# Sharing two of 64 dv stores unequally among the 16 DMA engines, and spreading six dk stores in place of seven, in an attention backward kernel bound by DMA

## The chip, the cores and the metric

The kernel runs on one core of a Trainium2 chip. The metric is the device time of one execution in microseconds, as the median of repeated runs. The core has 16 DMA engines. TensorE is PE in the profile (its weight loads are PEld), VectorE is DVE, ScalarE is ACT, GpSimd is POOL and SyncE is SP. The experiments had their own runs of the kernel before on the same chip, 9 to 11 of them per group, with medians of 1288.36, 1288.98, 1289.48, 1288.53 and 1289.18 us, so every measurement is given as a ratio as well. Differences between medians of different groups are good to 1 or 2 us: the 17.4 us below are 16.4 by the ratios.

## The reference

The reference is the forward and backward pass of attention with one query per head: 2 x 32 = 64 heads, 8192 keys, a head size of 128, all bf16.

```python
scores = jnp.einsum("bhqd,bhkd->bhqk", q, k) * q.shape[-1] ** -0.5
out = jnp.einsum("bhqk,bhkd->bhqd", softmax(scores), v)
# returned: out and the gradients dq, dk, dv for grad_out
```

With one query per head, dk and dv are outer products as large as k and v. Each head reads 2 MB of k and 2 MB of v, and writes 2 MB of dk and 2 MB of dv. That is 268 MB read and 268 MB written for very little arithmetic.

## The kernel before

A k or v tile has 128 rows (partitions) of 16 KB. SyncE issues all the big loads, on one queue; GpSimd issues all the big stores, on another. VectorE writes dk and dv over k and v in the same tile. There are 12 such tiles, six heads' worth, so a load must wait until the store of the tile's former owner has landed.

```python
def slot_of(i, w):          # w = 0: k, then dk; w = 1: v, then dv
    n = 2 * i + w
    return n if n < NTILE else slot_of(i - NTILE // 2, 1 - w)

def by_rows(eng, dst, src, rows):
    p = 0
    for m in rows:
        pin(eng.dma_start(out=dst[p : p + m], in_=src[p : p + m], max_dma_last_dim=NT * D))
        p += m
# ... (cut: load() issues the k or v tile of head i on SyncE)
            dst = (dv_v if w else dk_v)[i]
            if w == 0 and i in SPREAD:          # SPREAD = range(5, 64, 9): seven heads
                by_rows(store_eng, dst, h.tile[w], (P - 2, 2))
            else:
                pin(store_eng.dma_start(out=dst[:, b0:b1, :], in_=h.tile[w][:, b0:b1, :]))
```

So k of head i + 6 is loaded into the tile from which dv of head i is stored, and the wait stands in SyncE's program order.

The Trainium skill ("DMA: Bandwidth & Descriptors", section "Why a DMA increments its semaphore by 16 and not by 1") says that a transfer uses the largest number of engines, up to 16, that divides its outermost size. For GpSimd they are consecutive from a cursor that goes round; for SyncE they are the lowest-numbered ones. By that, 126 rows go to 14 engines with 9 rows each and the 2 rows that follow go to the remaining two, which so write 1 row where a plain store gives every engine 8. I call such a store a spread store. The packet records of the trace agree in number: 14 series of 18 half-row packets, and two engines without. The records carry no engine numbers, so every engine number in this document rests on that rule and on the cursor that the kernel sets to 6 at its start.

## Time and profile before

| | before |
|---|---|
| time, median of 3 runs | 1288.93 us (1288.64 to 1291.01) |
| HBM traffic over the span | 416 GB/s |
| last v load issued / last store issued | 1215.2 / 1279.0 us |
| landing of a 2 MB store / a k load | 67.1 / 21.1 us |

These lines are from the page of the kernel before: the rates in 40 equal slices, and the DMA issues with their size and the median time from issue to landing.

```profile
span 1290.8 us, 42577 instructions
...
DMA  9999999999999999999999999999999999999994
GB/s 390 423 427 428 427 427 426 428 427 427 427 427 428 428 426 425 412 429 426 428 426 427 427 426 428 428 426 424 426 427 428 426 421 424 427 429 426 421 383 185
...
HBM read 268.47 MB, written 268.47 MB: 416 GB/s over the span
...
out_dram<-kvt POOLq DMA_DIRECT2D x119, 2048.0 KB, 67.1
kvt<-in_v_dram SPq DMA_DIRECT2D x64, 2048.0 KB, 20.9
kvt<-in_k_dram SPq DMA_DIRECT2D x63, 2048.0 KB, 21.1
```

The rate stands near 427 GB/s from the third slice to the 38th (412 at the least), then falls to 383 and 185. One store and one load are issued about every 9.8 us, so by these landing times (67.1 / 9.8 and 21 / 9.8) some seven stores and two loads are in flight.

The waits view of the kernel before (waiting engine and line, what it waited for, us in total, times, longest):

```profile
PE tp L184 <- DMA kvt<-in_v_dram: 75.4, 43, 5.1
PE tp L184 <- DMA kvt<-in_k_dram: 23.7, 31, 2.0
```

SyncE's timeline of the kernel before around 500 us, and its last load (start, us, engine, line, transfer):

```profile
502.97 0.33 SPq L98 DMA_DIRECT2D kvt<-in_k_dram  x1
512.82 0.33 SPq L98 DMA_DIRECT2D kvt<-in_v_dram  x1
523.43 0.33 SPq L98 DMA_DIRECT2D kvt<-in_k_dram  x1
539.62 0.33 SPq L98 DMA_DIRECT2D kvt<-in_v_dram  x1
544.81 0.33 SPq L98 DMA_DIRECT2D kvt<-in_k_dram  x1
```

### The profile page before, as it was taken

Reading aid. Unit: us, or ns where it says so; the run is one execution under the profiler, and the core shown is the slowest. Engines: PE = TensorE matmul, PEld = TensorE weight load, DVE = VectorE, ACT = ScalarE, POOL = GpSimd, SP = SyncE. Lnnn points to the kernel's source line nnn. Section 1 sums busy time; section 2 is a strip of 40 time slices with the busy share of each in tenths; the row PEclk is TensorE's granted clock in tenths of the full one; section 3 lists DMA queues with packets and bytes.
Section 4 is the critical chain, followed back from the end, with each engine's and each line's share of the span. In section 5 each row is a group of like instructions: output and inputs, shape, how many; then the busy total and the mean of one; then the engine's idle time right before and its main releaser. Section 6 shows DMA issues by size and latency. Waiting matters only on the chain.

```text
span 1290.8 us, 42577 instructions
## 1 busy us (share of the span) xinstructions
PE 1126.7 (87%) x19268; PEld 856.4 (66%) x19268; DVE 936.1 (73%) x2122; ACT 975.1 (76%) x641; POOL 79.3 (6%) x150
## 2 busy tenths in 40 slices
PE   6999999988998988989888889899898888988870
PEld 5777777666676766766666667677666666766650
DVE  2888888777787777767667777677677776777780
ACT  6888888777787777777778777778687777877740
POOL 0000000000000000000000000000000000000000
PEclk9999999999999999989999998899899999999985
DMA  9999999999999999999999999999999999999994
GB/s 390 423 427 428 427 427 426 428 427 427 427 427 428 428 426 425 412 429 426 428 426 427 427 426 428 428 426 424 426 427 428 426 421 424 427 429 426 421 383 185
DMA packets 39985, 539.67 MB, mean 418 GB/s; under 512 B 5116, under 2 KB 5116, under 8 KB 6396
## 3 DMA queue, kind: packets, MB, share of 16 engines
q0 software_dynamic: 20784, 268.45, 49.4%
q1 hardware_dynamic: 19020, 268.51, 48.8%
q8 instruction: 150, 2.46, 0.7%
q14 instruction: 31, 0.25, 0.0%
HBM read 268.47 MB, written 268.47 MB: 416 GB/s over the span
## 4 chain that ended last, share of the span: by engine, by line
DMA 37%; another core or an unknown queue 27%; PE 20%; DVE 7%; issue 5%; ACT 1%; SPq 1%; POOL 0%; POOLq 0%; ACTq 0%
DMA kvt<-in_v_dram 17%; DMA kvt<-in_k_dram 13%; PE tp L184 9%; DMA out_dram<-kvt 6%; PE acc L339 5%; DVE kvt L394 4%; PE dpw L195 3%; PE sw L195 2%; DVE sel L362 1%; ACT ev L186 1%; SPq L98 1%; PE dpw L282 1%; DMA qd_nat<-in_q_dram 1%; DVE sel L356 0%
## 5 line engine op out<-in xcount | busy, mean ns | idle before, releaser
L186 ACT COPY ev<-tp 128x2048 bf16<-128x2048 bf16 x512 | 954.3, 1865 | 269.2 <-PE tp L184 257.6
L184 PE MATMUL tp<-ident_bf,kvt 128*128 128x128 bf16 x8192 | 556.0, 222 | 99.2 <-DMA kvt<-in_v_dram 75.4
L394 DVE TENSOR_TENSOR kvt<-qb,pair 128x2048 bf16<-128x2048 bf16 x512 | 621.4, 1214 | 0.3
L184 PEld LDWEIGHTS <-kvt 128*128 128x128 bf16 x8192 | 486.4, 100 | 106.7 <-DMA kvt<-in_v_dram 79.1
L195 PEld LDWEIGHTS <-ev 128*128 128x128 bf16 x8192 | 243.1, 96 | 208.1 <-issue 150.5
L339 PE MATMUL acc<-kvt,dS_pad 128*64 128x512 bf16 x1024 | 167.3, 409 | 1.6 <-DVE dqT L379 1.6
L339 PE MATMUL acc<-kvt,E_pad 128*64 128x512 bf16 x1024 | 160.5, 394 | 0.0
L195 PE MATMUL dpw<-qdT,ev 128*128 128x1 bf16 x4096 | 140.8, 164 | 17.6 <-DVE qb L177 16.6
L362 DVE SCALAR_TENSOR_TENSOR sel<-acc,diag,sel 128x128 f32<-128x128 f32 x384 | 134.7, 351 | 13.6
L195 PE MATMUL sw<-qdT,ev 128*128 128x1 bf16 x4096 | 141.8, 164 | 1.1 <-ACT ev L186 1.1
L411 POOL DMA_DIRECT2D out_dram<-kvt x127 | 68.0, 535 | 1121.0 <-DVE kvt L394 950.5
L207 DVE TENSOR_REDUCE mp<-sw 128x1 f32<-128x64 f32 x64 | 14.4, 224 | 149.7 <-PE sw L195 149.7
L339 PEld LDWEIGHTS <-dS_pad 128*64 128x64 bf16 x1024 | 37.6, 111 | 25.1 <-issue 5.1
L247 DVE CAST E_pad<-E_f 128x64 bf16<-128x64 f32 x64 | 12.5, 195 | 55.5 <-ACT E_f L238 55.5
L339 PEld LDWEIGHTS <-E_pad 128*64 128x64 bf16 x1024 | 36.3, 108 | 21.1 <-issue 0.4
L253 DVE CUSTOM_DVE_ANT_0 junk<-E_f,dpw 128x64 bf16<-128x64 f32 x64 | 14.1, 221 | 48.9 <-PE dpw L195 48.9
L376 PE MATMUL acc<-ones,sel 128*128 128x1 f32 x256 | 43.4, 239 | 6.2 <-DVE sel L362 6.2
L282 PE MATMUL dpw<-ld,ones 128*128 128x1 f32 x256 | 46.3, 250 | 0.1
L356 DVE TENSOR_SCALAR sel<-acc,diag 128x128 f32<-128x128 f32 x128 | 44.1, 344 | 0.0
L376 PEld LDWEIGHTS acc<-ones,sel 128*128 128x128 f32 x256 | 39.1, 193 | 7.3 <-DVE sel L362 7.3
L177 DVE CAST qb<-dpw 128x128 bf16<-128x128 f32 x128 | 35.5, 277 | 6.0 <-PE dpw L168 6.0
L282 PEld LDWEIGHTS dpw<-ld,ones 128*128 128x128 f32 x256 | 38.2, 189 | 0.5 <-DVE ld L253 0.5
(44 smaller groups left out, 313.3 us busy)
## 6 DMA issues: line engine op xcount, KB each, us to landing
out_dram<-kvt POOLq DMA_DIRECT2D x119, 2048.0 KB, 67.1
kvt<-in_v_dram SPq DMA_DIRECT2D x64, 2048.0 KB, 20.9
kvt<-in_k_dram SPq DMA_DIRECT2D x63, 2048.0 KB, 21.1
out_dram<-kvt POOLq DMA_DIRECT2D x7, 2016.0 KB, 70.6
out_dram<-kvt POOLq DMA_DIRECT2D x8, 512.0 KB, 22.2
kvt<-in_k_dram SPq DMA_DIRECT2D x2, 512.0 KB, 4.4
kvt<-in_k_dram SPq DMA_DIRECT2D x1, 1024.0 KB, 7.0
out_dram<-kvt POOLq DMA_DIRECT2D x7, 32.0 KB, 70.6
```

The lines of the kernel that those rows point to most:

```text
L177: pin(nc.vector.tensor_copy(out=h.qb[w][:], in_=h.qbp))
L184: pin(nc.tensor.transpose(tp[:, t, :], src[:, c * CH + t, :], ident_bf[:]))
L186: pin(nc.scalar.copy(out=ev[:], in_=tp[:]))
L195: nc.tensor.matmul(dst[:, c * CH + t : c * CH + t + 1], lhsT=ev[:, t, :], rhs=qdT[:, w, i : i + 1], start=True, stop=True,)
L207: pin(nc.vector.reduce_max(out=h.mp[:], in_=h.s, axis=AX.X))
L282: nc.tensor.matmul(out, lhsT=ones[:].to_broadcast([P, P]), rhs=col, start=True, stop=True)
L339: nc.tensor.matmul(h.acc[w][g : g + CW, :], lhsT=wts[:, n0 : n0 + CW], rhs=rows[:, n0 : n0 + QT, :].rearrange("p n d -> p (n d)"), start=( ...
L356: nc.vector.tensor_scalar(out=h.sel[:], in0=block, scalar1=diag[:, 0:1], scalar2=None, op0=ALU.mult)
L362: nc.vector.scalar_tensor_tensor(out=h.sel[:], in0=block, scalar=diag[:, b : b + 1], in1=h.sel[:], op0=ALU.mult, op1=ALU.add,)
L376: nc.tensor.matmul(h.acc[w][:, 0:1], lhsT=h.sel[:], rhs=ones[:], start=True, stop=True)
L394: nc.vector.tensor_tensor(out=h.tile[w][:, n0 : n0 + CH, :].rearrange("p n (e t) -> p n e t", t=2), in0=h.qb[w][:] .rearrange("p (e t) -> ...
L411: pin(store_eng.dma_start(out=dst[:, b0:b1, :], in_=h.tile[w][:, b0:b1, :]))
```

## The change

Engines do not come out even. By the reading of the packet records in the prediction below, eight of them also fetch instructions, which costs each some 25 us over the run (an estimate), and one engine is slow throughout. The intent of the change was to give more of two dv stores to engines thought to be free of that: 19 rows to each of the engines 14, 15 and 0 to 3, the rest to be shared so that the cursor comes out where it was. One dk spread store was dropped and the others moved.

```diff
-SPREAD = range(5, 64, 9)
+NARROW = (22, 44)
+SPREAD = range(7, 64, 10)
...
+    def narrow(dst, src):
+        m = 6 * 19
+        def eighths(ap, h):
+            parts = ap[P - 1 : P].rearrange("p (e h n) d -> p h e (n d)", e=8, h=2)
+            return parts[:, h]
+        pin(store_eng.dma_start(out=eighths(dst, 0), in_=eighths(src, 0)))
+        for r in (slice(0, m), slice(m, P - 1, P - 2 - m)):
+            pin(store_eng.dma_start(out=dst[r], in_=src[r], max_dma_last_dim=NT * D))
+        pin(load_eng.dma_start(out=eighths(dst, 1), in_=eighths(src, 1)))
+        for j in range(1, 5):
+            r = slice(m + j, P - 2, 4)
+            pin(load_eng.dma_start(out=dst[r], in_=src[r], max_dma_last_dim=NT * D))
...
-            if w == 0 and i in SPREAD:
+            if w == 1 and i in NARROW:
+                narrow(dst, h.tile[w])
+            elif w == 0 and i in SPREAD:
```

GpSimd stores half of the last row in eight pieces (to move the cursor by 8), then 114 rows on six engines, then 2 rows. SyncE stores the other half row and the 11 rows left over.

## The prediction

> **What bounds the kernel.** DMA traffic. The page's GB/s row stands near 427 in nearly every slice from 30 to 1,190 us, all 16 DMA engines busy; PE is busy 87%, ACT 76%, DVE 73%. 536.9 MB at 427 GB/s is 1,257 us; the remaining 34 us are the start (about 10) and the tail: the last two slices show 383 and 185 GB/s. Only the tail can be won, and it is set by the DMA engine that is latest with its own backlog.
>
> I read this from the trace's packet records. A 16 KB row packet takes 0.611 us, and the next on that engine starts 0.607 us later; until 1,240 us 16 packets are in flight, so they can be strung into 16 chains, one per engine:
> - Eight engines take the 150 instruction-fetch packets in turn. Each takes 0.97 us and stretches its neighbour to 0.98, so it costs about 1.3 us: some 25 us per engine over the run.
> - One of the two engines that the old spread stores relieve has packets of 0.63 to 0.65 us throughout: some 50 us.
> - The rest run clean. At the last spread store (head 59) they finish 32 us before the fetching ones, and one fetching engine is 7 us later still. At the end one engine alone writes for 6 us, after 10 us with 3 to 7 engines busy. Idle time after 1,240 us adds up to 276 engine-us: perfect balance can win 17 us.
>
> **What the change moves.** The Trainium skill ("DMA: Bandwidth & Descriptors", "Why a DMA increments its semaphore by 16 and not by 1") says that a transfer uses the largest count up to 16 that divides its outermost size, on consecutive engines from a cursor for GpSimd, on the lowest-numbered for SyncE. Before's packet sizes agree with 14 engines for 126 rows (18 half-row packets on 14 chains, 2 on two). By it, in 16 KB rows: engines 6 to 13 lose 17 each (-10.3 us); 3, 14, 15 gain 21 (+12.7), 2 gains 27, 0 and 1 gain 29 (+17.6); 4 and 5 lose 7 (-4.2). Bytes and compute are unchanged. This helps if the fetching engines are mostly 6 to 13; the clean ones have room (over 25 us). The records carry no engine numbers; I infer this from the change's intent, about 3 in 4. If fetching engines lie among 0 to 3, 14 and 15, the end moves about 10 us later.
>
> **Cost.** The narrow store's remainder goes through SyncE, in order: the next load (same buffer) waits until those rows land behind loads in flight (21 us to land). Loads pause 10 to 15 us twice. Stores in flight (67 us to land) should keep the engines busy; I charge 2 to 4 us in all.
>
> **Prediction.** Latest engine -10 us, cost +2 to +4: 1283 us; 8 in 10 between 1275 and 1296. Faster by over 2%: 0.02, within 2%: 0.95, slower: 0.03.
>
> **What will show it.** Right: the last two slices carry more than 383 and 185 GB/s, the lone engine's 6 us shrinks or goes, POOL's waits for earlier stores (128 us in the waits view) shrink, middle slices stay near 427. Wrong in the cost: dips near 450 and 880 us, more PE waiting for loads (79 us of weight-load waits on v). Wrong in the mapping: a longer last stretch with two to six engines in it.
>
> **What would make it wrong.** Fetching engines are numbered otherwise; the latest engine is 4 or 5; the pauses empty the queues.

## More of the kernel before

PE waits for loads often but never long: 5.1 us at most for v, 2.0 for k.

Windows of the kernel before, at the times where the change will act (window, its length, busy us and instructions of each engine, granted clock, DMA share, GB/s):

```profile
core 0: us, PE busy (x) PEld busy (x) DVE busy (x) ACT busy (x) POOL busy (x), PEclk, DMA share, GB/s
500.00:520.00 20.00, 17.88 (x307) 13.35 (x306) 15.14 (x34) 15.81 (x11) 1.06 (x2) 1.00 1.01 416
520.00:540.00 20.00, 18.23 (x302) 13.92 (x301) 14.28 (x34) 14.95 (x11) 1.07 (x2) 0.91 1.00 411
540.00:560.00 20.00, 16.87 (x282) 12.54 (x279) 13.81 (x32) 13.91 (x10) 1.06 (x2) 0.91 1.00 423
960.00:980.00 20.00, 17.20 (x286) 12.93 (x287) 13.78 (x34) 14.44 (x10) 1.06 (x2) 0.91 1.01 429
980.00:1000.00 20.00, 18.18 (x320) 13.96 (x316) 15.12 (x35) 15.61 (x12) 1.06 (x2) 1.00 1.01 427
```

Each window of 20 us has PE busy for 17 to 18 us and moves 411 to 429 GB/s.

```profile
1215.21 0.33 SPq L98 DMA_DIRECT2D kvt<-in_v_dram  x1
```

Loads leave about every 10 us. The gap of 16.2 us before 539.62 is the wait for the spread store of head 23; the loads' hold-up there is short.

## The result

The kernel after took 1302.55 us (1300.28 to 1303.98, 4 runs) against 1288.79 us (1288.62 to 1291.01, 4 runs) for the kernel before on the same chip: a ratio of 1.0101, 95% interval 1.0082 to 1.0120. Ratios here are the mean time of one kernel's runs over that of the other's in the same rounds, so not quite the ratio of the quoted medians. The time stayed within 2%, but it rose by 14 us where a fall of 6 was predicted, and lies outside the predicted range of 1275 to 1296.

The page of the kernel after, the same rows:

```profile
span 1300.2 us, 42601 instructions
...
DMA  9999999999999999999999999999999999999994
GB/s 389 425 426 427 427 425 427 429 426 428 428 426 426 429 424 397 413 412 424 422 427 426 429 426 423 406 429 415 404 405 398 422 427 426 429 425 424 425 414 191
...
HBM read 268.47 MB, written 268.47 MB: 413 GB/s over the span
...
out_dram<-kvt POOLq DMA_DIRECT2D x118, 2048.0 KB, 54.5
```

The row of rates has dips that the kernel before lacks: from the 16th slice (397, 413, 412) and from the 28th to the 31st (415, 404, 405, 398). They follow the narrow stores of heads 22 and 44, whose GpSimd parts are issued from 437 and from 889 us. The 26th slice (406, 813 to 845 us) comes before the second one; there the spread store of head 37 lands, at 834 us. The 39th slice is fuller (414 for 383) only because the whole program runs later. The DMA row still shows nines throughout: an engine that is counted busy is not an engine that is at its rate.

The waits view and the windows of the kernel after:

```profile
PE tp L202 <- DMA kvt<-in_v_dram: 59.3, 40, 6.6
PE tp L202 <- DMA kvt<-in_k_dram: 55.8, 33, 18.8
```

```profile
core 0: us, PE busy (x) PEld busy (x) DVE busy (x) ACT busy (x) POOL busy (x), PEclk, DMA share, GB/s
500.00:520.00 20.00, 18.98 (x338) 14.56 (x337) 15.92 (x39) 16.76 (x14) 0.00 (x0) 1.00 1.01 393
520.00:540.00 20.00, 1.22 (x24) 1.02 (x23) 2.10 (x5) 1.59 (x1) 1.60 (x3) 0.55 0.99 404
540.00:560.00 20.00, 17.37 (x265) 12.77 (x264) 11.78 (x27) 12.61 (x7) 0.53 (x1) 0.85 1.01 424
960.00:980.00 20.00, 14.58 (x258) 11.05 (x254) 14.14 (x31) 13.83 (x10) 2.50 (x4) 0.99 1.01 363
980.00:1000.00 20.00, 7.88 (x104) 5.94 (x105) 4.27 (x12) 4.49 (x3) 0.00 (x0) 0.59 1.00 411
```

PE now waits up to 18.8 us for one k load. In the window from 520 us PE is busy for 1.22 us of 20 while DMA still moves 404 GB/s: nearly everything that moves there is stores. From 980 us the same comes again. SyncE's timeline of the kernel after shows why, and its last load:

```profile
493.43 0.33 SPq L116 DMA_DIRECT2D kvt<-in_v_dram  x1
493.85 2.24 SPq L103 DMA_DIRECT2D out_dram<-kvt  x1
496.14 6.89 SPq L106 DMA_DIRECT2D out_dram<-kvt  x4
522.28 0.34 SPq L116 DMA_DIRECT2D kvt<-in_k_dram  x1
526.64 0.34 SPq L116 DMA_DIRECT2D kvt<-in_v_dram  x1
```

```profile
1229.77 0.33 SPq L116 DMA_DIRECT2D kvt<-in_v_dram  x1
```

After the SyncE share of the narrow store, at 496.1 us, the next k load is issued only at 522.3: it waits for the narrow store to land, whose GpSimd part lands at 521.8. The second time the gap is from 949.5 to 974.1 us; GpSimd's part has then landed at 960.0, and the rest of the wait is for SyncE's own share. The last load of the program is issued at 1229.8 us, 14.6 us later than before.

### The profile page after: what moved, and what is told of

It reads as the page before. It is cut to its first block, busy times and chain, and to the rows that moved or that the text cites. A ratio compares the mean times of both kernels' runs of the same rounds, so it can differ in the third digit from the quotient of the medians.

```text
span 1300.2 us, 42601 instructions
## 1 busy us (share of the span) xinstructions
PE 1121.4 (86%) x19268; PEld 853.6 (66%) x19268; DVE 935.7 (72%) x2122; ACT 975.7 (75%) x641; POOL 82.1 (6%) x153
## 2 busy tenths in 40 slices
DMA packets 40996, 539.68 MB, mean 415 GB/s; under 512 B 5970, under 2 KB 6002, under 8 KB 7282
## 4 chain that ended last, share of the span: by engine, by line
DMA 44%; PE 19%; another core or an unknown queue 17%; issue 9%; DVE 6%; SPq 1%; ACT 1%; POOL 1%; POOLq 0%; ACTq 0%
DMA kvt<-in_v_dram 29%; PE tp L202 9%; DMA kvt<-in_k_dram 7%; DMA out_dram<-kvt 7%; PE acc L357 5%; DVE kvt L412 4%; PE sw L213 2%; PE dpw L213 2%; DVE sel L380 1%; ACT ev L204 1%; SPq L116 1%; PE dpw L300 1%; DMA qd_nat<-in_q_dram 1%; SPq L106 0%
## 5 line engine op out<-in xcount | busy, mean ns | idle before, releaser
L265 DVE CAST E_pad<-E_f 128x64 bf16<-128x64 f32 x64 | 12.5, 196 | 54.2 <-ACT E_f L256 54.2
```

## How the loss was followed through the experiments

Besides the times, two readings of the packet records serve as measures. Packet times are counted from the first packet and run some 10 to 11 us later than the span's clock.

First, the time from the start of the last load packet to the end of the last store packet is the same in nearly all kernels: 49.0 to 54.2 us in 17 of the 20 profiles (all but e5, e6 and e7, which change late stores; below). In these 17 the end of the program is therefore the last load plus some 50 us, and most of what they differ by is the time of the last load.

What is left for the latest engine shows in the time from the issue of the last load to the end of the span, in one profile each: 75.6 us before (1290.8 - 1215.2), 65.5 in e1 (1282.8 - 1217.3), 70.4 after (1300.2 - 1229.8). At the end of the kernel before one engine writes alone for some 6 us, in e1 for 0.3, after for 1.9. So the tail did become shorter, as the prediction hoped, but it does so by 10.1 us in e1, without any narrow store. Against e1 the narrow stores lengthen the tail by 4.9 us and delay the last load by 12.5: together the 17.4 us that they cost.

Second, the loads have pauses. This is what each queue moved, in GB/s, SyncE's queue (loads, and in the kernel after its share of the narrow stores) first and GpSimd's stores second, in steps of 4 us (e1, g2 and f2 are experiments; e1 has no narrow stores):

```
us         e1        g2        f2       after
512    221 209   287 143   238 178   197 209
516    188 238    98 307    57 338   114 293
520    225 193   111 320     0 399    19 371
524    221 221   221 205     0 403    20 358
528    205 201   193 225     0 420     8 365
532    221 213   238 205     8 389    12 381
536    209 225   213 197   176 213   168 205
...
972    233 195   213 221    20 385    39 389
976    242 184   258 170     0 231    25 365
980    238 186   225 197     0 186    16 311
984    201 219   225 197     0 147     8 338
988    250 176   233 184   106  68    94 182
```

While both queues have work, each gets about half, 213 GB/s. The Trainium skill ("DMA: Bandwidth & Descriptors", section "Queues, rings and completion order") says that an engine goes round the queues that have work, packet by packet, which agrees. When loads stop, stores take 360 to 420 GB/s, so the total hardly falls. But when loads resume they soon get about their half again and no more, so the time is not made up. In f2's second pause stores run out too, and 186 and 147 GB/s is all that moves.

The table of all kernels, ordered by the last load packet. "Pauses" sums the stretches of at least 7 us in which the load queue moved under 60 GB/s, in one profile each.

| kernel | dv stores of heads 22 and 44 | median us | ratio to before | last load us | pauses us |
|---|---|---|---|---|---|
| g3 | one heavy engine, 2 then 3 | 1286.19 | 0.9983 | 1240.8 | 14 |
| e1 | plain | 1285.12 | 0.9974 | 1241.6 | 0 |
| f3 | plain, five spread stores | 1286.54 | 0.9972 | 1241.8 | 0 |
| g2 | one heavy engine, 0 then 1 | 1285.70 | 0.9987 | 1243.7 | 0 |
| e7 | the change, at heads 58 and 60 | 1300.46 | 1.0093 | 1243.9 | 0 |
| before | plain, seven spread stores | 1288.79 | 1 | 1244.3 | 0 |
| e8 | four equal transfers | 1289.82 | 1.0005 | 1246.2 | 0 |
| e2 | 16 of 128 rows by SyncE | 1291.98 | 1.0031 | 1248.4 | 20 |
| f4 | plain, four spread stores | 1293.12 | 1.0022 | 1249.1 | 0 |
| g4 | 19 rows on one half, then on the other | 1298.88 | 1.0079 | 1252.7 | 25 |
| after | the change | 1302.55 | 1.0101 | 1257.2 | 33 |
| h2 | 19 rows on five engines, in place of two spread stores | 1302.88 | 1.0106 | 1258.0 | 28 |
| g1 | one heavy engine, 14 then 15 | 1302.98 | 1.0116 | 1261.3 | 18 |
| e3 | 18 rows on 14, 15, 0 to 3 | 1307.95 | 1.0151 | 1262.5 | 26 |
| h1 | 19 rows on 15, 0 to 3 | 1308.51 | 1.0149 | 1265.1 | 29 |
| e4 | 18 rows on 6 to 11 | 1307.25 | 1.0148 | 1265.2 | 30 |
| f1 | 19 rows on 14, 15, 0 to 3, and SyncE | 1315.29 | 1.0193 | 1271.0 | 29 |
| f2 | one heavy engine, 6 | 1321.27 | 1.0235 | 1275.9 | 36 |

The two kernels e5 and e6 are left out. Every kernel with a last load after 1250 us has 18 to 36 us of pauses; those before have none, but for e2 with 20 and g3 with 14, which are two stretches just at the threshold of 7. The correlation of the two columns is 0.85 and the slope 0.66 us per us. Long pauses are thus the larger part of the delay, but not all of it, and this part of the argument is a correlation over one profile of each kernel.

How a pause begins can be read directly. Up to the dv store of head 22, issued at some 437 us, the following kernels do what e1 does. Given are, on the span's clock, when the last GpSimd part of that store landed and when SyncE issued the next load, that of k of head 28 into the same tile:

| | e1 | g2 | g3 | e8 | h1 | e3 | e4 | g4 | f1 | after | g1 | f2 |
|---|---|---|---|---|---|---|---|---|---|---|---|---|
| landed, us | 503.4 | 507.9 | 508.9 | 510.2 | 514.1 | 517.0 | 519.3 | 519.9 | 521.0 | 521.8 | 522.0 | 522.9 |
| next load, us | 503.4 | 508.1 | 509.1 | 510.4 | 514.3 | 517.2 | 519.4 | 520.0 | 521.1 | 522.3 | 522.2 | 523.1 |

The load leaves within 0.5 us of the landing in all of them. GpSimd stops as well: in no profile does it issue a transfer before the one eight issues earlier has landed. In the kernel after it waits 26.2 us for that, until 522.2 us, so a late store holds up the loads and the stores behind it alike.

## The experiments

### e1_spread6: the spread stores alone

```diff
-SPREAD = range(5, 64, 9)
+SPREAD = range(7, 64, 10)
```

> Only the other half of the change: six spread stores at heads 7, 17, ... 57 in place of seven, no narrow store. Every theory: about as before, 1287 to 1293 us (engines 4 and 5 get 7 rows more, 4.2 us, and neither is the latest; the other 14 get 1 row less). If it comes out near 1302, the six spread stores are the cause and none of the narrow-store theories is needed.

Measured: 1285.12 us, ratio 0.9974 (0.9961 to 0.9988). The half of the change that concerns dk saves 3 us, a little more than expected; the narrow stores therefore cost 17.4 us (1302.55 - 1285.12). All the kernels that follow except f3 and f4 build on e1.

### e2_pause: a SyncE share without unequal shares

```diff
-SPREAD = range(5, 64, 9)
+NARROW = (22, 44)
+SPREAD = range(7, 64, 10)
...
+            if w == 1 and i in NARROW:
+                by_rows(store_eng, dst, h.tile[w], (P - 16,))
+                pin(load_eng.dma_start(out=dst[P - 16 :], in_=h.tile[w][P - 16 :], ...))
-            if w == 0 and i in SPREAD:
+            elif w == 0 and i in SPREAD:
```

> Six spread stores, and the dv stores of heads 22 and 44 split evenly: 112 rows from GpSimd and 16 rows (one per engine) from SyncE, so all engines carry 8 rows as ever, but the next load stands behind a SyncE store in SyncE's queue as in the change. Theory pause (the loads' pause empties the queues): near the changed kernel, 1297 to 1304, with dips of GB/s near 500 and 950 us and a gap of 25 to 30 us between two load issues. Theory mapping (the 19-row engines include instruction-fetching ones, which become the latest): as e1, 1287 to 1293, whatever the gap.

Measured: 1291.98 us, ratio 1.0031 (1.0019 to 1.0044), 6.9 us over e1. That is inside the range of the theory of the map and below that of the pause. The wait in SyncE's order is a real cost, but under half of 17.4 us.

### e3_narrow_gp: unequal shares without SyncE

```diff
-SPREAD = range(5, 64, 9)
+NARROW = (22, 44)
+SPREAD = range(7, 64, 10)
...
+            if w == 1 and i in NARROW:
+                by_rows(store_eng, dst, h.tile[w], (8, 102, 2, 16))
-            if w == 0 and i in SPREAD:
+            elif w == 0 and i in SPREAD:
```

> Six spread stores, and the narrow stores from GpSimd alone: 8 rows on engines 6 to 13, 102 rows on 14, 15, 0 to 3 (17 each), 2 on 4 and 5, 16 on all: 18 rows on the six, 2 on the ten. No SyncE store, so no pause of loads by SyncE. Theory mapping: the six gain 20 less 1 rows = 19 (11.5 us), so near the changed kernel less some: 1296 to 1303. Theory pause: as e1, 1287 to 1293. The intent (fetching engines are 6 to 13): 1278 to 1285. A third theory, that the extra GpSimd transfers take up its eight semaphores and make POOL wait for earlier stores, expects POOL waits of over 20 us at heads 22 and 44 here too and a time over 1293.

Measured: 1307.95 us, ratio 1.0151 (1.0137 to 1.0165). With nothing left to SyncE the loss is larger, not smaller: 22.8 us over e1, and above every range given. Only the third theory, the wait of GpSimd for earlier stores, named a time over 1293; that wait is 19.3 us at head 22, just under its 20.

### e4_narrow_6to11: the other six engines

```diff
-SPREAD = range(5, 64, 9)
+NARROW = (22, 44)
+SPREAD = range(7, 64, 10)
...
+            if w == 1 and i in NARROW:
+                by_rows(store_eng, dst, h.tile[w], (102, 10, 16))
-            if w == 0 and i in SPREAD:
+            elif w == 0 and i in SPREAD:
```

> As e3, but the 18-row engines are 6 to 11 (102 rows first, then 10 rows, then 16). If fetching engines are 6 to 13 or 5 to 12 (the intent), this is far the worst: 1300 to 1310, and e3 the best. If the fetching engines are 13 to 15 and 0 to 4, this is the best: 1278 to 1285. If they are every other engine, e4 and e3 come out alike, within 3 us, both slower than e1, because three fetching engines are among the six in both.

Measured: 1307.25 us, ratio 1.0148 (1.0134 to 1.0162), the same as e3. The prediction's map of good and bad engines cannot be right as a choice between these two sixes.

### e5_even and e6_odd: which half of the engines is late

Both are e1 with seven late stores (heads 58 to 61) cut into three transfers; e5 has (96, 23, 9), e6 has (96, 9, 23).

```diff
+LATE = [(i, w) for i in range(58, 62) for w in (1, 0)][:7]
...
+            if (i, w) in LATE:
+                by_rows(store_eng, dst, h.tile[w], (96, 23, 9))     # e6: (96, 9, 23)
```

> e1, plus seven late stores (dv and dk of heads 58 to 60, dv of 61, whose buffers no load follows, so no load can be held up): 96 rows on all engines, 23 on one engine, 9 on the next nine. The cursor then moves by 10, so the heavy engines are 6, 0, 10, 4, 14, 8, 2: every second engine; each ends about 13 rows (8 us) heavier than in e1, the odd ones about 10 rows lighter. Theory mapping with even engines fetching instructions: 1291 to 1300. With odd ones fetching: 1276 to 1283. If fetching has no parity (6 to 13, or 13 to 4): both of this pair about alike. The theory of pauses alone expects both near e1, 1285 plus or minus 3.

> As e5, with the 9 rows before the 23, so the heavy engines are 15, 9, 3, 13, 7, 1, 11: seven odd ones, all but 5. Theory mapping with even engines fetching: 1276 to 1283, the best so far. With odd ones fetching: 1291 to 1300. Sequence and sizes of transfers are otherwise those of e5, so the difference of the two is the mapping alone.

Measured: 1328.63 us (ratio 1.0315) and 1323.71 us (1.0268). These two miss. Their last loads lie at 1242.3 and 1243.3 us, as in e1, but the end comes 95.4 and 86.4 us after them: the last stores are held up, since GpSimd waits for the transfer eight issues earlier to land before it issues one. Whether that is due to the 14 extra transfers or to the one heavy engine in each store, these runs do not separate. The 5 us between the two kernels say nothing sure about engines.

### e7_narrow_late: the change where no load follows

```diff
-NARROW = (22, 44)      # of the kernel after
+NARROW = (58, 60)
```

> The changed kernel with its two narrow stores moved from heads 22 and 44 to 58 and 60, where no load follows into the buffer: same rows on the same engines, no load can wait for them. Theory mapping alone (three of the 19-row engines fetch): as slow as the changed kernel, 1298 to 1306, since the latest engine has the same rows. Theory pause alone (loads held up twice): as e1, 1283 to 1289. Both at work: in between, and the split between them is read off: the middle of the run lost 12.8 us against e1 and the tail 3.8 by my count of idle and stretched packets in the changed kernel's trace, so I lean to 1289 to 1300.

Measured: 1300.46 us, ratio 1.0093 (1.0077 to 1.0109). No load waits for these stores, yet only 2 us are saved, as the theory of the map alone expected. The loads are not late: these are the last loads of e1 and of e7, and GpSimd's issues after the narrow store of head 60 (last, in brackets, its idle time and what the view takes to have ended it).

```profile
1217.31 0.33 SPq L98 DMA_DIRECT2D kvt<-in_v_dram  x1
```

```profile
1217.04 0.33 SPq L116 DMA_DIRECT2D kvt<-in_v_dram  x1
```

```profile
1238.77 1.12 POOL L431 DMA_DIRECT2D out_dram<-kvt  x2 [19.33 <-DVE sel L380]
```

The last load packet starts at 1243.9 us, 2 us later than e1's, but the end comes 63.3 us after it. GpSimd stands still for 19.3 us. The view puts that down to VectorE, which was long done; the transfer eight issues earlier, the 114 rows of head 58, landed at 1238.2 us, 76 us after its issue, and GpSimd issues 0.6 us later. So unequal shares cost about as much where they can only hold up other stores: 15.3 us over e1 here.

### e8_split4: four transfers, equal shares

```diff
-SPREAD = range(5, 64, 9)
+NARROW = (22, 44)
+SPREAD = range(7, 64, 10)
...
+            if w == 1 and i in NARROW:
+                by_rows(store_eng, dst, h.tile[w], (32, 32, 32, 32))
-            if w == 0 and i in SPREAD:
+            elif w == 0 and i in SPREAD:
```

> e1, with the dv stores of heads 22 and 44 cut into four GpSimd transfers of 32 rows, two per engine each: no imbalance and no SyncE store, only more transfers in GpSimd's eight semaphores. Theory that the count of transfers matters: over 1290, with POOL waits over 15 us at those heads. Theories pause and mapping: as e1, 1284 to 1287.

Measured: 1289.82 us, ratio 1.0005 (0.9990 to 1.0021), 4.7 us over e1. Six more transfers cost about 0.8 us each. The unequal shares of e3, which has as many transfers, cost the other 18 us.

### f1_cursor_right: the intended placement

In the trace of the kernel after, the spread store of head 37 relieves another pair of engines than those of heads 7, 17 and 57, so the first narrow store had moved the cursor by 8 engines against the intent. (The slow engine gives it away: among the half-row packets of the spread stores of heads 27 and 37, 19 and 14 took 313 to 360 ns, where 309 is the rule, and only 2 to 4 at heads 7, 17 and 57.) f1 replaces the one-row pieces.

```diff
-SPREAD = range(5, 64, 9)
+NARROW = (22, 44)
+SPREAD = range(7, 64, 10)
...
+            if w == 1 and i in NARROW:
+                by_rows(store_eng, dst, h.tile[w], (8, 114, 2))
+                pin(load_eng.dma_start(out=dst[P - 4 :], in_=h.tile[w][P - 4 :], ...))
-            if w == 0 and i in SPREAD:
+            elif w == 0 and i in SPREAD:
```

> six spread stores plus, for heads 22 and 44, dv by GpSimd in 8 rows (one on each of 8 engines), 114 rows (19 on each of 6) and 2 rows, and 4 rows by SyncE. The 8 one-row pieces of the change are gone, so a cursor that moves by 8, 6 and 2 ends where it started and the 19 rows lie on engines 14, 15 and 0 to 3. Theory mapping (the change fails because its one-row pieces moved the cursor 8 engines too far, so that fetching engines got the 19 rows and spread stores 27 and 37 relieved the wrong pair): 1280 to 1288, clearly under after's 1302. Theory unequal shares (whichever six engines are heavy, the store lands late and the light engines run out of transfers): 1299 to 1308, as e3's 1308. Either way the pair relieved at head 37 should be the same as at heads 7, 17 and 57.

Measured: 1315.29 us, ratio 1.0193 (1.0174 to 1.0212). The pair relieved is the same at all spread stores, as intended, and the kernel is 12.7 us slower than the change and above both ranges. The misplaced cursor was not the cause; g4 suggests that it even helped. The loss is about the sum of e3's 22.8 and e2's 6.9 us.

### f2_one_heavy: one engine instead of six

```diff
-SPREAD = range(5, 64, 9)
+NARROW = (22, 44)
+SPREAD = range(7, 64, 10)
...
+            if w == 1 and i in NARROW:
+                by_rows(store_eng, dst, h.tile[w], (96, 17, 15))
-            if w == 0 and i in SPREAD:
+            elif w == 0 and i in SPREAD:
```

> six spread stores plus, for heads 22 and 44, dv by GpSimd in 96, 17 and 15 rows: 17 is prime, so one engine carries 23 rows and the fifteen others 7 each, and the cursor ends where it started. The bytes are nearly as even as in e8 for fifteen engines, but the transfer lands as late as the one heavy engine lets it. Theory late landing (the next transfers and the next load wait for the heavy engine, so all others starve): 1296 to 1305, e8's 1290 and 8 or more. Theory number of light engines (what is lost is the work that the light engines lack at that moment): 1288 to 1293, as e8.

Measured: 1321.27 us, ratio 1.0235 (1.0210 to 1.0260), the slowest of those with narrow stores at heads 22 and 44, and above both ranges. Since fifteen engines carry 7 rows each, it is not a matter of how many engines are light. The windows of f2:

```profile
core 0: us, PE busy (x) PEld busy (x) DVE busy (x) ACT busy (x) POOL busy (x), PEclk, DMA share, GB/s
960.00:980.00 20.00, 13.26 (x230) 10.17 (x229) 12.78 (x27) 12.44 (x9) 1.00 (x3) 0.89 0.63 245
980.00:1000.00 20.00, 5.59 (x56) 4.01 (x56) 1.97 (x7) 2.24 (x2) 1.59 (x3) 0.51 0.98 385
```

From 960 us DMA is at 0.63 of its share and 245 GB/s: with loads stopped, the stores in flight are used up and PE makes no new ones. The half-row packets show two groups of engines. At head 22 one group starts on this store at 487 to 497 us, the other at 502 to 511, so the second lags by some 15 us. The last engine is still writing the heavy rows alone until 532 us. It belongs to the late group.

### f3_spread5 and f4_spread4: fewer spread stores

```diff
-SPREAD = range(5, 64, 9)
+SPREAD = range(9, 64, 12)      # f3; f4: range(11, 64, 14)
```

> only the spread stores, five of them (heads 9, 21, 33, 45, 57). If each spread store costs some 2 to 4 us of interrupted streams, as the step from seven (1289.0) to six (1285.1) says: 1281 to 1284. If the relief of the slow pair is what counts: the slow engine gains 18 rows (11 us) and ends last: 1286 to 1292.

> only the spread stores, four of them (heads 11, 25, 39, 53). Cost of each spread store alone: 1277 to 1282. Relief lost: the slow engine lags by 22 us against six: 1292 to 1305.

Measured: 1286.54 us (ratio 0.9972, 0.9958 to 0.9987) and 1293.12 us (1.0022, 1.0004 to 1.0041). Five are as good as six. With four, 8 us are lost against e1 without one long pause, as expected if the slow pair is no longer relieved enough. So balance between engines does matter, as the prediction held.

### g1_heavy_14_15, g2_heavy_0_1, g3_heavy_2_3: the heavy engine moved

The theory by then was this: rows put on an engine that is already late hold up the whole store; rows put on an early one do not.

```diff
-SPREAD = range(5, 64, 9)
+NARROW = (22, 44)
+SPREAD = range(7, 64, 10)
...
+            if w == 1 and i in NARROW:
+                k = {22: 8, 44: 9}[i]      # g1
+                by_rows(store_eng, dst, h.tile[w], (96, k, 17, 15 - k))
-            if w == 0 and i in SPREAD:
+            elif w == 0 and i in SPREAD:
```

In g2 k is 10 and 11, in g3 12 and 13. The heavy engine is the one k past the cursor.

> f2 with its heavy engine elsewhere: dv of heads 22 and 44 by GpSimd in 96, k, 17 and 15-k rows, so that one engine carries 23 rows and fifteen carry 7, with k = 8 (engine 14) at head 22 and k = 9 (engine 15) at head 44, if the cursor starts at 6. Four transfers as e8. Theory latest engine (only rows on engines that are already behind cost): if both engines are of the early group, 1288 to 1294, near e8's 1290; if one of the two is late, 1297 to 1308. Theory late landing whichever engine is heavy: 1316 to 1324, as f2's 1321.

> the same with k = 10 (engine 0) at head 22 and k = 11 (engine 1) at head 44. Latest engine: 1288 to 1294 if both are early, 1297 to 1308 if one is late. Late landing whichever is heavy: 1316 to 1324. By the latest-engine theory at most one of the kernels g1, g2 and g3 is over 1296.

> the same with k = 12 (engine 2) at head 22 and k = 13 (engine 3) at head 44. Latest engine: 1288 to 1294 if both are early, 1297 to 1308 if one is late. Late landing whichever is heavy: 1316 to 1324.

Measured: g1 1302.98 us (ratio 1.0116, 1.0101 to 1.0130), g2 1285.70 (0.9987, 0.9974 to 0.9999), g3 1286.19 (0.9983, 0.9971 to 0.9995). The transfers have the same sizes in all three and in nearly the same order, and 17 us lie between them: a heavy engine may cost nothing or 17 us. The store of head 22 lands at 522.0 us in g1 and at 507.9 and 508.9 in g2 and g3, and the next load leaves 0.2 us later each time. In g1 the half-row packets show the heavy engine of head 22 writing alone until 531 us, as in f2. At head 44 just 14 such packets come late and alone (958 to 971 us): that is the share of a light engine (12 of the 96 rows' packets and 2 more), where a heavy one has 46. So the late engine is read to be the one 8 past the cursor, number 14. In g2 the last such packet at head 22 starts at 516.5 us, in g3 at 518.6. Four of the six engines that the change meant to load are thus read to be early, and one is late; the numbers are inferred.

The page of g2, and SyncE's timeline where the kernel after had its gap:

```profile
GB/s 388 421 427 428 428 425 429 428 427 427 426 429 427 427 426 418 425 429 420 428 428 428 428 427 422 423 427 426 419 419 427 424 428 427 428 428 425 422 405 244
```

```profile
493.61 0.33 SPq L99 DMA_DIRECT2D kvt<-in_v_dram  x1
508.10 0.33 SPq L99 DMA_DIRECT2D kvt<-in_k_dram  x1
513.21 0.33 SPq L99 DMA_DIRECT2D kvt<-in_v_dram  x1
```

The load after that of 493.61 follows 14.5 us later; in the kernel after it came 28.9 us after that of 493.43. And the rates dip only to 418 and 419.

### g4_alternate: each half once

```diff
-SPREAD = range(5, 64, 9)
+NARROW = (22, 44)
+SPREAD = range(7, 64, 10)
...
+            if w == 1 and i in NARROW:
+                by_rows(store_eng, dst, h.tile[w], (8, 114, 2) if i == 22 else (114, 8, 2))
+                pin(load_eng.dma_start(out=dst[P - 4 :], in_=h.tile[w][P - 4 :], ...))
-            if w == 0 and i in SPREAD:
+            elif w == 0 and i in SPREAD:
```

> f1 with the second narrow store mirrored: head 22 in 8, 114 and 2 rows as f1, head 44 in 114, 8 and 2 rows, so that the 19 rows fall on engines 14, 15 and 0 to 3 the first time and on 6 to 11 the second; 4 rows by SyncE both times. Latest engine: no engine gets the extra 11 rows (6.7 us) twice, so the latest engine is 6.7 us less late than in f1, and what that costs is less by 6.7 to 12 us: 1303 to 1309. Any narrow store costs the same wherever it falls: 1313 to 1317, as f1.

Measured: 1298.88 us, ratio 1.0079 (1.0066 to 1.0092), 16.4 us under f1 and better than the range given. f1's pauses in the packets are 17 and 12 us; here they are 18 and 7. The first store, the same as f1's, costs the same; the second, on the half that the first left early, costs less. That the change's cursor slipped by 8 after its first narrow store, so that its two stores fell on different halves, is a possible reason why it is faster than f1. That this accounts for the 12.7 us is argued from g4, not shown.

### h1_five_heavy and h2_five_instead: only the early engines

h1 leaves engine 14 out of the six.

```diff
-SPREAD = range(5, 64, 9)
+NARROW = (22, 44)
+SPREAD = range(7, 64, 10)
...
+            if w == 1 and i in NARROW:
+                by_rows(store_eng, dst, h.tile[w], (9, 85, 2, 32))
-            if w == 0 and i in SPREAD:
+            elif w == 0 and i in SPREAD:
```

> six spread stores plus dv of heads 22 and 44 by GpSimd in 9, 85, 2 and 32 rows: engines 6 to 14 and 4, 5 carry 3 rows each, 15 and 0 to 3 carry 19 each, as many as in the change and in f1, but engine 14 is among the light ones. Cursor returns to 6. Theory one late engine (14): the five early engines take 13 us more over the two stores, within their lead, the late ones lose 6 us, four transfers cost what e8's do (4.7): 1281 to 1288. Theory unequal shares as such: 1303 to 1316, as e3 and f1.

h2 has such stores of dk at heads 27 and 47 in place of two of the six spread stores.

```diff
+NARROW = (27, 47)
...
-                by_rows(store_eng, dst, h.tile[w], (P - 2, 2))
+                by_rows(store_eng, dst, h.tile[w], (9, 85, 2, 32) if i in NARROW else (P - 2, 2))
```

> six such stores of dk at heads 7, 17, 27, 37, 47, 57, of which 27 and 47 are in 9, 85, 2 and 32 rows and the others in 126 and 2: the two uneven stores take the place of two spread stores, so only four transfers more than six spreads have, not six. Slow pair relieved almost as by a spread store (3 rows in place of 1), late engines lose 6 rows each against it per store (7.3 us in all), four more transfers cost about 3 us: 1280 to 1284, the fastest. If relief of the late engines is worth nothing because something else sets the time of the last load: 1285 to 1289.

Measured: h1 1308.51 us (ratio 1.0149, 1.0128 to 1.0170), h2 1302.88 (1.0106, 1.0089 to 1.0123). Both miss: one late engine is not the whole explanation. These are the rows of rates of h1 and h2, in that order:

```profile
GB/s 389 422 428 428 426 426 427 428 427 427 429 426 427 425 415 400 426 426 419 423 427 428 427 428 425 424 429 408 405 364 420 413 420 427 428 427 425 424 356 162
```

```profile
GB/s 389 422 427 428 428 424 430 426 427 428 428 426 428 426 428 428 427 427 397 417 426 428 426 427 423 422 426 429 426 419 414 375 427 427 427 428 426 423 380 158
```

In h1 the second narrow store (364 GB/s in the 30th slice) hurts more than the first (400 in the 16th); in h2 likewise (397 in the 19th, 375 in the 32nd). By the packets the pauses are 10 and 19 us in h1, 10 and 18 in h2. At the second store of h1 most of the half-row packets come at 930 to 976 us and hardly any before 914, while in e8 an early group is plain from 907 to 923: by this reading, which no run tests, the five engines had lost their lead. What stays open is why already the first of these stores pauses the loads for 10 us while the first of g2's and of g3's, whose single heavy engine has 23 rows instead of 19, pause them for under 7. In h1 the load after the store was issued at 514.3 us, in g2 at 508.1, and GpSimd waited 15.3 us for the 85-row transfer to land. Whether it is the five engines together, or the other eleven running dry, no run here tells.

## Why the prediction was wrong

**What bounds the kernel, and "only the tail can be won".** DMA bounds it: right. But the tail was not the only thing that could move, nor was it mainly "set by the DMA engine that is latest with its own backlog". In 17 profiles the end comes 49.0 to 54.2 us after the last load packet, while it moves by 36 us. What counts most there is when the last load is through. The latest engine has a smaller part, up to 10 us between the kernel before and e1, and late stores can hold up the end by themselves (e7).

**The map ("This helps if the fetching engines are mostly 6 to 13").** The packet rule held: f2's 17 rows ran on one engine. As far as it was tested, the map was mostly right (0 to 3 early, 6 and 14 late) and still no help: engine 14 among the heavy six is late (g1 against g2 and g3), and if it was the transfer in 8 pieces that the cursor did not count, the first narrow store's 19 rows fell on 6 to 11, with 6 among them. The sign named for a wrong map came: at the end two to six engines are at work for 13.7 us, before for 3.8, in e1 for 2.5. That the late engines are the ones that fetch instructions was not tested. The prediction gave one chance in four to a wrong map and expected a loss of 10 us from it; one late engine in one store, g1, costs 17 us over g2. The cursor slip was not foreseen, but placing it right made the kernel slower (f1).

**"Latest engine -10 us".** This step failed. The tail after the issue of the last load became 5.2 us shorter, but e1 alone makes it 10.1 us shorter; what the narrow stores themselves did to it was +4.9 us, in one profile each. The step adds up rows over the run as if the order did not matter. By the experiments it does: a store that lands late holds up the next load and GpSimd's next store at once. At the time of the store, an engine with 19 rows in the queue takes them alternately with load packets: 11 more rows take 11 x 2 x 0.61 = 13 us of wall time (an estimate from the packet time), which is about all of the lead of 15 us at head 22, if the engine has that lead, and a delay for everybody if it has not (g2 and g3 against g1). No kernel with narrow stores was faster than e1, not even h2, where the rows went to engines read as early. Why h1 and h2 lose as much as they do stays open. At most g2 and g3, at 0.9987 and 0.9983 against e8's 1.0005 with as many transfers, hint at a gain from relief, and a small one.

**"Stores in flight (67 us to land) should keep the engines busy; I charge 2 to 4 us in all".** This term was mis-sized by a factor of about four: the narrow stores delay the last load by 12.5 us of the 17.4 that they cost. The picture behind it was half right. Stores did keep the engines busy (404 GB/s in the window from 520 us), but of the wrong kind: in those 17 and 16 us of pause hardly any load moved, loads got about half afterwards, and the last load came at 1257.2 us for e1's 1241.6. The named sign of a wrong cost, dips near 450 and 880 us with PE waiting more for loads, came, though at 520 and 970 us and for k instead of v, because it is k of head i + 6 that waits for dv of head i.

**What was right.** The SyncE share does stop the loads (e2: 6.9 us), and the prediction's fear that "the pauses empty the queues" is what f2's 147 GB/s shows. The prediction did not cost the change of the spread stores by itself; e1 shows it to be worth 3 us.

The fastest versions measured are e1 and f3, 0.9974 and 0.9972 of the time before: the change without its narrow stores.

## What to carry to other kernels

Where loads wait in program order for stores, a transfer is as late as its last engine, and every load behind it waits; before rows are shared unequally, find out which engines are behind at that moment, and count the extra rows twice if another queue takes turns on the same engine. A busy DMA row does not show a loss: look at loads and stores apart, because a pause in the one that feeds the computation is not made up later by a queue that only gets its half. If the lead of early engines is to be spent, g4 and h1 suggest spending it once and on different engines. And try the plainest part of a change alone: here that was the whole gain.

## What the Trainium skill lacked or had wrong

- "DMA: Bandwidth & Descriptors", section "Why a DMA increments its semaphore by 16 and not by 1": its rule for the number of engines held for 126, 96 and 17 rows, but by it the change's transfer in 8 pieces of one row should move the cursor by 8 and return it to its place; in the trace the pair relieved at heads 27 and 37 differs from that at 7, 17 and 57 (19 and 14 slow half-row packets for 2 to 4). The transfer did use 8 engines: the 5970 packets under 512 B fit that by the next point, where 16 engines would make 5954. With 8 whole rows in f1 the pair stays the same. Why the cursor slipped is open.
- The same section says that all 16 engines report the completion of a GpSimd transfer, but not what else the runs show: an engine that the transfer does not use gets one packet of 4 bytes for every packet of one that it uses. The profile's count of packets under 512 B is 5036 in e1 and 5956 in f1. Of the 920 more, completion writes are 72 (16 for each of four more GpSimd transfers, 4 for each of two SyncE transfers on four engines); the other 848 are 2 x (8 x 2 + 10 x 38 + 14 x 2), idle engines times half rows for the 8, 114 and 2 rows. The same sum gives the counts of e2, e3, e4, e8, f2, g1 and h1 to the packet. They take 9 ns each; no run here tells whether they cost anything.
- The same page, section "Latency and other measured facts", says that engines 7 and 15 are usually slower. Here, by the reading in the prediction, one engine of the pair that the spread stores relieve (4 and 5, if the cursor stands at 6) has packets of 0.63 to 0.65 us for the others' 0.611, and no run singles out 7 or 15. By the same reading eight engines fetch instructions, 150 packets in turn, which costs each 25 us by the prediction's estimate; no page gives what such fetches take from an engine's share of the data.
- No page says that rounds between queues make a pause of one of them a lasting delay: loads and stores had about 213 GB/s each in e1 and after the pauses, with 360 to 420 for stores within them.
